# Convolution and SwiGLU on one core: output copies shared by two engines, taps and conversion jobs moved

## The chip, the cores and the metric

The kernel runs on one core of one Trainium2 chip. A core has five engines that run side by side, each with its own queue of instructions in program order: TensorE (PE in the profile; PEld is its weight load), VectorE (DVE), ScalarE (ACT), GpSimd (POOL) and SyncE (SP), which here only issues transfers. PSUM is the small memory into which TensorE writes, SBUF the large one from which it reads; transfers (DMA) run on engines of their own and are issued from SP and POOL.

The metric is device time in microseconds (us), the median of several executions. Before the change it is 792.96 us, over 3 runs from 792.71 to 793.93.

## What is computed

A causal convolution over time with 7 taps, whose weights are a softmax per head, and then a gated feed-forward layer on its output:

```python
def _attn_ref(x, weight):                 # x [8, 4096, 192], weight [8 heads, 7 taps]
    w = np.exp(weight - weight.max(-1, keepdims=True))
    w = w / (w.sum(-1, keepdims=True) + 1e-09)
    x_pad = np.concatenate([zeros(B, 6, D), x], axis=1)
    # out[b, s, head, g] = sum over k of w[head, k] * x_pad[b, s + k, head, g]
    ...

def _moe_ref(x, w_gate, w_val, w_out):    # x [32768, 192], d_ff 1536
    g = x @ w_gate
    silu = g * (1.0 / (1.0 + np.exp(-g)))
    return (silu * (x @ w_val)) @ w_out
```

Inputs and output are float32; the kernel works in float16 with float32 accumulation.

## The kernel before

**Blocks, chunks, steps.** The 32768 tokens are 64 blocks of 512 (`TB`). The feed-forward width of 1536 is 12 chunks of 128. One step of the main loop (line 886) is one chunk of one block: step `n` = 12 x block + chunk `j`, 768 steps. Four blocks are a unit (`u`, 48 steps), 16 units in all.

**A step.** `gate_val(n)` (line 757) multiplies the convolved input `xc[b]` (three tiles of 128 rows, the third dimension `k`) by the weights of that chunk: three pairs of 64-row matmuls, gate and val side by side, into one PSUM tile each, three buffers per name. ScalarE takes `silu` of gate (L775), VectorE multiplies it by val into `h` (L777), 15 buffers.

**Slots.** After chunks 1, 4, 7 and 10 a slot of `down` matmuls (L792) adds `h` times the output weights into two accumulator banks, `acc0` and `acc1`, which have one buffer each. The slot behind chunk 7 (`slot(1)`, 24 matmuls) takes the h of chunks 0 to 5 of its own block, the one behind 10 (36) chunks 0 to 8, the one behind chunk 1 of the next block (24) chunks 6 to 11, the one behind chunk 4 (12) chunks 9 to 11. With this last one the block is done: ScalarE copies both banks to `o_sb` (L850, L851), and SP stores it (L854). So the newest h that a slot needs is that of two steps before, and the slot behind 4 needs none that is new.

**Where the convolved input comes from.** Units 0, 1, 4, 7, 10 and 13 are convolved on TensorE, with a band matrix (`conv_half`, two halves of 32 matmuls, each in a slot behind chunk 10; for unit 1 at steps 25 and 31; unit 0 by smaller pieces at the start), casts to SBUF, a store to a scratch in DRAM and transposing fetches (`fetch`, L520, three per block). The others (`POOLED`: 2, 3, 5, 6, 8, 9, 11, 12, 14, 15) are convolved tap by tap on the other engines. `cast_x` writes a unit's input as float16 to DRAM (POOL's queue, L586), `turn_x` reads it back transposed (SP's queue, L601; 528 columns, two names of tiles with 6 buffers each), `join_x` puts two halves into one tile (L605). Six jobs make a unit (`conv_job`): block 0, pair 0, block 1, pair 1, block 2, block 3. A job is 7 taps: ScalarE writes the first into `total` and another into `part` (L676), VectorE adds two to `total` (`dve_step`, L651), and then GpSimd adds the part and the last three (L641, L626), and writes the result. `place` (L700) copies the results of jobs into the tiles `t1` and `t2` of a block by four SP transfers.

**What sets the order.** Everything is written out by hand: `seq` keeps the order of calls on each engine. `planned` (line 716) gives each unit the steps for its cast, its turns and its jobs: units 2 and 3 by a table, the others 118 and 95 steps before their first. `pooled_work` (line 732) runs at the end of each step: VectorE's next tap behind chunks 4 and 10, and behind 1 and 7 when VectorE's job is behind ScalarE's; ScalarE's next tap behind chunks 1, 7 and 10, up to two jobs ahead of VectorE. A block is placed 14 steps after its last job was issued and not before 16 steps ahead of its use. An instruction's place in its queue is what these steps fix; when it runs, its waits decide. SP and POOL have no tie to a step other than such waits.

**Tap weights per channel.** `make_picks` (step 24) makes two selection masks of 8 x 128 with GpSimd iotas and four VectorE operations; `make_channel_taps` (step 33) uses them in four small matmuls and one ScalarE copy into `both_taps`.

Of the kernel before, what the change touches and what calls it, by code (L numbers as in the profile page):

```python
# [10 lines left out]
def kernel(  # L11
# [9 lines left out]
    nc = tc.nc  # L21
    fp32 = mybir.dt.float32
    fp16 = mybir.dt.float16
    i32 = mybir.dt.int32
    AF = mybir.ActivationFunctionType
    ALU = mybir.AluOpType
# [5 lines left out]
    H, K = weight.shape  # L32
    NT = B * S
    Dff = moe_w_gate.shape[1]
    P = 128
    Q = 64
    SL = D // Q
    grp = D // H
    SUBS = 4
    TB = P * SUBS  # L40
# [32 lines left out]
    def seq(i):  # L73

        e = i.ins.engine
        if e in last_on:
            tc.add_manual_dep(i.ins, last_on[e].name, NOSYNC, reason="order")
        last_on[e] = i.ins
        return i

    wpool = ctx.enter_context(tc.tile_pool(name="wts", bufs=1))
    cpool = ctx.enter_context(tc.tile_pool(name="conv", bufs=2))
# [29 lines left out]
    def xe_tile(e):  # L112
        xe[e] = cpool.tile([P, 6, D], fp16, tag="xe", name="xe", bufs=4)
# [62 lines left out]
    def load_wo(m):  # L176
        seq(
            nc.gpsimd.dma_start(
                out=wo16[:, E * m : E * m + E, :].rearrange("p e d -> p (e d)"),
                in_=moe_w_out[WF * m : WF * m + WF, :].rearrange(  # L180
                    "(p e) d -> p (e d)", p=P
                ),
            )
        )

    def small(name, shape, dt=fp32):
        return wpool.tile(shape, dt, tag=name, name=name)
# [14 lines left out]
    load_w(2)  # L202
    for m in range(3):
        load_wo(m)
    xe_tile(2)
    xe_load(2)
    xe_tile(3)
# [32 lines left out]
    def make_shift(n):  # L240
# [26 lines left out]
            op=ALU.mult,  # L267
# [8 lines left out]
            op0=ALU.mult,  # L276
            op1=ALU.subtract,
# [249 lines left out]
    XP = 16  # L527
# [6 lines left out]
    pick = {}  # L534

    def make_picks():
        for name, first, rows in (("c01", 0, P), ("c2", P, Q)):
            which = small(f"which_{name}", [H, P], i32)
            seq(
                nc.gpsimd.iota(  # L540
                    which,
                    pattern=[[0, P // rows], [1, rows]],
                    base=first,
                    channel_multiplier=-grp,
                )
            )
            low = small(f"low_{name}", [H, P])
            seq(nc.vector.tensor_single_scalar(low, which, 0, op=ALU.is_ge))
            pick[name] = small(f"pick_{name}", [H, P], fp16)
            seq(  # L550
                nc.vector.scalar_tensor_tensor(
                    pick[name], which, float(grp), low, op0=ALU.is_lt, op1=ALU.mult
                )
            )

# [40 lines left out]
    def turn_x(u, i, at):  # L596
        rows = xs[u][TB * i : TB * i + TB + XP]
        tiles = (x01, x12)[at // Q]
        tag = f"x{at // Q}"
        t = cpool.tile([P, TB + XP], fp16, tag=tag, name=tag, bufs=6)  # L600
        seq(nc.sync.dma_start_transpose(out=t, in_=rows[:, at : at + P]))  # L601
        tiles[u, i] = t

# [111 lines left out]

    def planned(v):
        s0 = ustep * v
        cast, jobs = {2: (19, 44), 3: (40, 60)}.get(v, (s0 - 118, s0 - 95))
        turns = (
            (0, 0), (0, Q), (2, Q), None, (1, 0), (1, Q), (3, Q), None, (2, 0), (3, 0)  # L720
        )
        lead = {2: (33, 1), 3: (49, 1)}.get(v, (cast + 7, 2))
        plan.setdefault(cast, []).append(lambda: cast_x(v))
        for m, turn in enumerate(turns):
            if turn:
                todo = lambda turn=turn: turn_x(v, *turn)
            else:
                todo = lambda i=m // 4: join_x(v, i)
            plan.setdefault(lead[0] + lead[1] * m, []).append(todo)
        plan.setdefault(jobs, []).append(lambda: queue_jobs(v))  # L730

    def pooled_work(n, j, busy):
        step_now[0] = n
        if not busy:
            ready = dve_steps[0][0] if dve_steps else None
            ahead = act_steps[0][0] if act_steps else n_jobs[0]
            if ready is not None and (
                j in (4, 10) or (j in (1, 7) and ready < ahead)
            ):
                dve_steps.pop(0)[1]()  # L740
            if j in (1, 7, 10) and act_steps and (ready is None or ahead < ready + 3):
                act_steps.pop(0)[1]()
        while placing:
            u, i = placing[0]
            need = (u, "block", i), (u, "pair", i % 2)
            if not all(job in finished for job in need):
                break
            done = max(finished[job] for job in need)
            if n < max(done + 14, ustep * u + NCH * i - 16):
                break  # L750
            placing.pop(0)
            place(u, i)
# [27 lines left out]
    acc = {}  # L780
# [44 lines left out]
    def slot(k, b, after=None, between=None):  # L825

        if k == 1:
            acc[b] = [
                apool.tile([P, 2, D], fp32, tag=f"acc{i}", name=f"acc{i}")
                for i in range(2)  # L830
            ]
            down(b, [(False, G[0])], 1, after)
            if between is not None:
                between()
            down(b, [(False, G[1])], 1, None)
        elif k == 2:
            down(b, [(True, G[0]), (True, G[1])], 0, after)
            if between is not None:
                between()
            if b < n_blocks - 1:  # L840
                down(b, [(False, G[2])], 0, None)
        elif k == 3:
            down(b, [(True, G[2])], 1, after)
            if between is not None:
                between()
            down(b, [(False, G[3])], 1, None)
        else:
            down(b, [(True, G[3])], 0, after)
            o_sb = hpool.tile([P, SUBS, D], fp32, tag="o_sb", name="o_sb", bufs=3)
            seq(nc.scalar.copy(o_sb[:, 0:2, :], acc[b][0]))  # L850
            seq(nc.scalar.copy(o_sb[:, 2:4, :], acc[b][1]))  # L851
            t0 = b * TB
            seq(
                nc.sync.dma_start(  # L854
                    out=out[t0 : t0 + TB, :].rearrange("(s p) d -> p s d", p=P),
                    in_=o_sb,
                )
            )
            del acc[b]
# [26 lines left out]
    for n in range(n_steps):  # L886
        b, j = divmod(n, NCH)
        u, ls = divmod(n, ustep)
        work = None
        if n in (12, 19):  # L890

            def work(e=2 if n == 12 else 3):
                early(e, (gate_bank, gate_bank, val_bank))

        at = (25, 31) if u == 0 else (10, 22)
        if u + 1 < NU and not pooled(u + 1) and ls in at:

            def work(u=u, hh=at.index(ls)):
                conv_half(u + 1, hh)

        gate_val(n)
        if n == 6:
            early(1, (*acc_banks, gate_bank))
        elif n == 8:
            eturn(1, (*acc_banks, gate_bank))
        elif n in (9, 12, 15, 17):
            k = {9: 1, 12: 2, 15: 3, 17: 4}[n]
            slot(k, 0, silu[n - 1 if k == 4 else n - 2], work)
        elif j % 3 == 1 and n > 18:
            k = {1: 3, 4: 4, 7: 1, 10: 2}[j]  # L910
            slot(k, b - 1 if j < 7 else b, silu[n - 2], work)
        if n == 18:
            eturn(2, (*acc_banks, gate_bank))
        elif n == 20:
            eout(3)
        elif n == 21:
            efetch(3)
        if n == 24:
            make_picks()
        if n == 33:  # L920
            make_channel_taps()
        for job in plan.pop(n, ()):
            job()
        pooled_work(n, j, work is not None)
        if u + 1 < NU and not pooled(u + 1):
            if ls == at[0]:
                conv_dup(u + 1)
            if ls == at[1]:
                for m in range(2):
                    conv_out(u + 1, m)  # L930
            if ls == at[1] + 1:
                for m in range(2, 8):
                    conv_out(u + 1, m)
            lo = 32 if u == 0 else 28
            if ls in range(lo, lo + 12, 3):
                fetch(UB * (u + 1) + (ls - lo) // 3)
        if u + 2 < NU and not pooled(u + 2):
            if ls == (21 if u == 0 else 1):
                x16_tile(u + 2)
                load_x(u + 2, 0, silu[n - 1])  # L940
            if ls == (23 if u == 0 else 5):
                load_x(u + 2, 1, silu[n - 1])
            if ls == (37 if u == 0 else 26):
                dup_x(u + 2)
    b = n_blocks - 1
# [41 lines left out]
```

## Time and profile before

| | |
|---|---|
| median of 3 runs | 792.96 us |
| the profiled execution | 793.59 us |
| its span, from the first instruction to the last | 791.8 us |
| TensorE clock granted in it | 0.999 |
| busy: PE, DVE, ACT, POOL | 775.6, 638.4, 588.6, 500.7 us |

The profile is one execution. A busy share is a mean over the whole span, so stretches with different limits are mixed in it: units with tap jobs load DVE, ACT and POOL, the others hardly load POOL. The page's groups give, per line of the kernel, the engine, the shapes out<-in, the count, the busy time, the mean duration of one in ns, and the idle time of the engine just before such an instruction with what ended most of it. The chain is the work that ended last, followed back from the end: each piece has its start, its length, its engine and line, and x and the number of instructions merged in it. A timeline lists one engine's instructions with start and length, and in square brackets the idle time before and what ended it; for SP the length is that of issuing the transfer, not of moving the data. All times count from the start of the span.

### The profile page before, as it was taken

To read this page: it belongs to the slowest core of one execution; us is meant where nothing else is said; L and a number is where in the kernel's file an instruction comes from. 1 tells how busy PE (TensorE), PEld (TensorE's weight loads), DVE (VectorE), ACT (ScalarE), POOL (GpSimd) and SP (SyncE) were. 2 spreads that over 40 slices of the span, in tenths; PEclk is the share of its full clock that TensorE was granted. 3 is DMA by queue.
4 is the path that set the end of the run, shared out by engine and by line. 5 is a ranking of instruction groups with operands and counts; after the bars stand their busy time and mean duration, and the time that the engine had idled before them with its cause. 6 is when DMAs were issued, how large, how long until landed. Compare 5 with 4: busy or idle time off the path is not lost.

```text
span 791.8 us, 27799 instructions
## 1 busy us (share of the span) xinstructions
PE 775.6 (98%) x11371; PEld 521.7 (66%) x11371; DVE 638.4 (81%) x949; ACT 588.6 (74%) x1054; POOL 500.7 (63%) x485
## 2 busy tenths in 40 slices
PE   8999999999999999999999999999999999999997
PEld 5666666666666666666666666666666666666665
DVE  6677889888888867888896688898767888886665
ACT  6677787877878767777876678788668787876664
POOL 8102999996899920589995047899802689990000
PEclk9999999999999999999999999999999999999999
DMA  9965538355642394386129638631862653221211
GB/s 140 177 141 99 124 106 166 83 123 129 115 109 69 56 201 109 94 130 133 39 68 174 117 83 155 107 92 46 146 144 78 150 123 76 68 64 40 68 55 41
DMA packets 159840, 83.90 MB, mean 106 GB/s; under 512 B 102552, under 2 KB 159136, under 8 KB 159136
## 3 DMA queue, kind: packets, MB, share of 16 engines
q1 hardware_dynamic: 139216, 65.58, 35.4%
q0 software_dynamic: 20496, 16.54, 15.0%
q8 instruction: 89, 1.46, 0.8%
q14 instruction: 39, 0.32, 0.1%
HBM read 33.08 MB, written 38.60 MB: 91 GB/s over the span
## 4 chain that ended last, share of the span: by engine, by line
PE 94%; DVE 2%; issue 1%; SPq 1%; DMA 0%; ACT 0%; DVEq 0%; ACTq 0%
PE gate L766 60%; PE acc L792 30%; DVE h L777 2%; PE val L766 2%; PE cv L462 1%; PE warm L867 1%; DMA x<-xs 0%; SPq L520 0%; PE turn L431 0%; PE cv L373 0%; SPq L498 0%; PE acc L813 0%; ACT tme L391 0%; ACT wide L331 0%; ACT sig L775 0%
## 5 line engine op out<-in xcount | busy, mean ns | idle before, releaser
L777 DVE TENSOR_TENSOR h<-sig,val 128x512 f16<-128x512 f16 x768 | 500.0, 685 | 143.5 <-PE val L766 123.1
L775 ACT ACTIVATE sig<-gate 128x512 f16<-128x512 f32 x768 | 455.3, 599 | 183.0 <-PE val L766 155.9
L766 PEld LDWEIGHTS <-w 64*128 64x128 f16 x4608 | 255.6, 110 | 182.3 <-issue 1.5
L766 PE MATMUL val<-pxc,w 64*128 64x512 f16 x1440 | 337.2, 376 | 0.0
L766 PE MATMUL gate<-pxc,w 64*128 64x512 f16 x1440 | 337.2, 376 | 0.0
L792 PE MATMUL acc<-wo,h 64*128 64x192 f16 x6096 | 300.4, 243 | 9.8 <-DVE h L777 7.9
L792 PEld LDWEIGHTS <-h 64*128 64x128 f16 x6096 | 257.7, 94 | 73.9 <-DVE h L777 13.3
L766 PE MATMUL val<-xc,w 64*128 64x512 f16 x864 | 203.6, 376 | 0.3 <-DVE h L777 0.3
L766 PE MATMUL gate<-xc,w 64*128 64x512 f16 x864 | 203.6, 376 | 0.0
L626 POOL TENSOR_TENSOR total<-total,piece 128x512 f32<-128x512 f32 x120 | 158.4, 1320 | 10.0
L641 POOL TENSOR_SCALAR piece<-x,both_taps 128x512 f32<-128x512 f16 x180 | 146.1, 812 | 0.0
L651 DVE SCALAR_TENSOR_TENSOR total<-x,both_taps,total 128x512 f32<-128x512 f16 x120 | 130.4, 1087 | 0.0
L626 POOL TENSOR_TENSOR total<-total,part 128x512 f32<-128x512 f32 x60 | 81.0, 1349 | 69.6 <-DVE total L651 53.9
L490 POOL COPY tm<-tm 128x1280 f16<-128x1280 f16 x5 | 6.2, 1249 | 125.5 <-DVE tm L479 125.5
L626 POOL TENSOR_TENSOR pxc<-total,piece 128x512 f16<-128x512 f32 x40 | 55.8, 1396 | 3.3
L676 ACT ACTIVATE total<-x,both_taps 128x512 f32<-128x512 f16 x60 | 42.8, 714 | 2.6 <-DMA x<-xs 2.6
L676 ACT ACTIVATE part<-x,both_taps 128x512 f32<-128x512 f16 x60 | 42.8, 714 | 0.0
L851 ACT COPY o_sb<-acc 128x384 f32<-128x384 f32 x63 | 30.6, 486 | 0.0
L850 ACT COPY o_sb<-acc 128x384 f32<-128x384 f32 x63 | 30.2, 479 | 0.1
L626 POOL TENSOR_TENSOR y<-total,piece 128x512 f16<-128x512 f32 x20 | 25.7, 1287 | 1.7
L479 ACT CAST tm<-cv 128x480 f16<-128x480 f32 x20 | 10.2, 562 | 6.8 <-PE cv L462 6.8
L479 DVE CAST tm<-cv 128x480 f16<-128x480 f32 x20 | 12.2, 651 | 0.5
(68 smaller groups left out, 88.4 us busy)
## 6 DMA issues: line engine op xcount, KB each, us to landing
out_dram<-o_sb SPq DMA_DIRECT2D x63, 384.0 KB
pxc<-pxc SPq DMA_DIRECT2D x80, 64.0 KB
pxc<-y SPq DMA_DIRECT2D x80, 64.0 KB
x<-in_x_dram POOLq DMA_DIRECT2D x10, 480.0 KB, 9.7
scr<-tm SPq DMA_DIRECT2D x35, 130.0 KB
xs<-in_x_dram POOLq DMA_DIRECT2D x5, 774.0 KB, 7.0
xs<-in_x_dram POOLq DMA_DIRECT2D x5, 768.0 KB, 10.4
x<-x SPq DMA_DIRECT2D x8, 480.0 KB
```

The costliest lines, as they stand in the source:

```text
L462: nc.tensor.matmul(banks[r][32 * c : 32 * c + 32, t * w : t * w + w], band[Q * r : Q * r + Q, h, :], x16[u][Q * r : Q * r + Q, NG * c : NG ...
L479: eng(tm[u][:, NG * r : NG * r + NG, 2 * grp * hp : 2 * grp * hp + 2 * grp].rearrange("p g (t e) -> p g t e", t=2), banks[r][:, 0 : 2 * w] ...
L626: nc.gpsimd.tensor_tensor(job["dst"] if k == K - 1 else total, total, part, op=ALU.add)
L641: nc.gpsimd.tensor_scalar(part, shifted(k), scalar1=job["tap"][:, k : k + 1], scalar2=1.0, op0=ALU.mult, op1=ALU.mult,)
L651: nc.vector.scalar_tensor_tensor(job["total"], shifted(k), job["tap"][:, k : k + 1], job["total"], op0=ALU.mult, op1=ALU.add,)
L676: nc.scalar.activation(part, shifted(k), AF.Copy, scale=job["tap"][:, k : k + 1])
L766: nc.tensor.matmul(o, w16[m][p0 : p0 + Q, k, e::E], xc[b][k][p0 : p0 + Q, 0:TB], start=(k == 0), stop=(k == SL - 1),)
L775: silu[n] = seq(nc.scalar.activation(sg, g, AF.Silu)).ins
L777: seq(nc.vector.tensor_tensor(hj, sg, v, op=ALU.mult))
L792: nc.tensor.matmul(acc[b][bank][:, s, :], hj[p0 : p0 + Q, ts(2 * bank + s, P)], wo16[p0 : p0 + Q, j, :], start=(not second and j == 0 and ...
L850: seq(nc.scalar.copy(o_sb[:, 0:2, :], acc[b][0]))
L851: seq(nc.scalar.copy(o_sb[:, 2:4, :], acc[b][1]))
```

## The change

Five edits:

- **Output copy.** Of the two copies of a finished block's banks, the second goes from ScalarE to VectorE (`nc.vector.tensor_copy`), for the 63 blocks before the last.
- **Taps.** VectorE's taps stand behind chunks 1, 7 and 10, whenever one is ready; none behind chunk 4. ScalarE's condition is as before.
- **Picks.** The two iotas of `make_picks` and the first compare, now on GpSimd, move to the loads at the start, ahead of the input of blocks 2 and 3 and unit 1. What is left (two VectorE operations) moves from step 24 to 34, `make_channel_taps` from 33 to 37.
- **Steps of the jobs.** Unit 2: cast 19 to 21, first turn 33 to 42, jobs 44 to 54. Unit 3: cast 40 to 50, first turn 49 to 60 with two steps between turns in place of one, jobs 60 to 72. All others: 6 steps later.
- **Buffers.** The transposed input has 8 buffers per name in place of 6.

```diff
--- before.py
+++ after.py
@@ -202,6 +202,20 @@
     load_w(2)
     for m in range(3):
         load_wo(m)
+    which = {}
+    above = {}
+    for name, first, rows in (("c01", 0, P), ("c2", P, Q)):
+        which[name] = small(f"which_{name}", [H, P], i32)
+        seq(
+            nc.gpsimd.iota(
+                which[name],
+                pattern=[[0, P // rows], [1, rows]],
+                base=first,
+                channel_multiplier=-grp,
+            )
+        )
+        above[name] = small(f"above_{name}", [H, P])
+        seq(nc.gpsimd.tensor_single_scalar(above[name], which[name], 0, op=ALU.is_ge))
     xe_tile(2)
     xe_load(2)
     xe_tile(3)
@@ -534,22 +548,12 @@
     pick = {}
 
     def make_picks():
-        for name, first, rows in (("c01", 0, P), ("c2", P, Q)):
-            which = small(f"which_{name}", [H, P], i32)
-            seq(
-                nc.gpsimd.iota(
-                    which,
-                    pattern=[[0, P // rows], [1, rows]],
-                    base=first,
-                    channel_multiplier=-grp,
-                )
-            )
-            low = small(f"low_{name}", [H, P])
-            seq(nc.vector.tensor_single_scalar(low, which, 0, op=ALU.is_ge))
+        for name in which:
             pick[name] = small(f"pick_{name}", [H, P], fp16)
             seq(
                 nc.vector.scalar_tensor_tensor(
-                    pick[name], which, float(grp), low, op0=ALU.is_lt, op1=ALU.mult
+                    pick[name], which[name], float(grp), above[name],
+                    op0=ALU.is_lt, op1=ALU.mult,
                 )
             )
 
@@ -597,7 +601,7 @@
         rows = xs[u][TB * i : TB * i + TB + XP]
         tiles = (x01, x12)[at // Q]
         tag = f"x{at // Q}"
-        t = cpool.tile([P, TB + XP], fp16, tag=tag, name=tag, bufs=6)
+        t = cpool.tile([P, TB + XP], fp16, tag=tag, name=tag, bufs=8)
         seq(nc.sync.dma_start_transpose(out=t, in_=rows[:, at : at + P]))
         tiles[u, i] = t
 
@@ -715,11 +719,11 @@
 
     def planned(v):
         s0 = ustep * v
-        cast, jobs = {2: (19, 44), 3: (40, 60)}.get(v, (s0 - 118, s0 - 95))
+        cast, jobs = {2: (21, 54), 3: (50, 72)}.get(v, (s0 - 112, s0 - 89))
         turns = (
             (0, 0), (0, Q), (2, Q), None, (1, 0), (1, Q), (3, Q), None, (2, 0), (3, 0)
         )
-        lead = {2: (33, 1), 3: (49, 1)}.get(v, (cast + 7, 2))
+        lead = {2: (42, 1), 3: (60, 2)}.get(v, (cast + 7, 2))
         plan.setdefault(cast, []).append(lambda: cast_x(v))
         for m, turn in enumerate(turns):
             if turn:
@@ -734,9 +738,7 @@
         if not busy:
             ready = dve_steps[0][0] if dve_steps else None
             ahead = act_steps[0][0] if act_steps else n_jobs[0]
-            if ready is not None and (
-                j in (4, 10) or (j in (1, 7) and ready < ahead)
-            ):
+            if j in (1, 7, 10) and ready is not None:
                 dve_steps.pop(0)[1]()
             if j in (1, 7, 10) and act_steps and (ready is None or ahead < ready + 3):
                 act_steps.pop(0)[1]()
@@ -848,7 +850,7 @@
             down(b, [(True, G[3])], 0, after)
             o_sb = hpool.tile([P, SUBS, D], fp32, tag="o_sb", name="o_sb", bufs=3)
             seq(nc.scalar.copy(o_sb[:, 0:2, :], acc[b][0]))
-            seq(nc.scalar.copy(o_sb[:, 2:4, :], acc[b][1]))
+            seq(nc.vector.tensor_copy(o_sb[:, 2:4, :], acc[b][1]))
             t0 = b * TB
             seq(
                 nc.sync.dma_start(
@@ -915,9 +917,9 @@
             eout(3)
         elif n == 21:
             efetch(3)
-        if n == 24:
+        if n == 34:
             make_picks()
-        if n == 33:
+        if n == 37:
             make_channel_taps()
         for job in plan.pop(n, ()):
             job()
```

In the changed kernel a line's number is up to 14 higher than before (L601 becomes L605, L777 becomes L779).

## Prediction

> **What bounds the kernel.** The page's table of engines comes first, then the chain that ended last and the costliest groups.
>
> ```profile
> PE 775.6 (98%) x11371; PEld 521.7 (66%) x11371; DVE 638.4 (81%) x949; ACT 588.6 (74%) x1054; POOL 500.7 (63%) x485
> ...
> PE 94%; DVE 2%; issue 1%; SPq 1%; DMA 0%; ACT 0%; DVEq 0%; ACTq 0%
> ...
> L777 DVE TENSOR_TENSOR h<-sig,val 128x512 f16<-128x512 f16 x768 | 500.0, 685 | 143.5 <-PE val L766 123.1
> ...
> L651 DVE SCALAR_TENSOR_TENSOR total<-x,both_taps,total 128x512 f32<-128x512 f16 x120 | 130.4, 1087 | 0.0
> ...
> L851 ACT COPY o_sb<-acc 128x384 f32<-128x384 f32 x63 | 30.6, 486 | 0.0
> ```
>
> PE sets the end at full clock, so only what makes PE wait counts. The chain in order of time, blocks 27 to 29, shows where:
>
> ```profile
> 352.27 1.49 PE acc L792 x36
> 355.70 0.99 PE acc L792 x24
> 358.63 0.49 PE acc L792 x12
> 361.16 0.47 issue
> 361.63 0.69 DVE h L777
> 362.36 0.34 PE acc L792 x4
> 364.64 1.49 PE acc L792 x36
> ```
>
> The x36 piece comes once a block (behind chunk 10). Undisturbed, it returns after 11.73 us; here after 12.37, since the slot behind chunk 7 waited for the h of chunk 5. DVE's timeline has a 1.81 us tap at 359.90, behind chunk 4. I took the start of every step (first gate matmul in PE's timeline) and compared each chunk with its undisturbed length (0.65 us; 1.64 with the slots behind 1 and 7, 1.14 behind 4, 2.13 behind 10). From block 5 on, every excess over 0.06 us, apart from the 32-matmul convolution halves (0.64 each), is at chunk 7 and follows a tap behind chunk 4 longer than 1.165 us: 24 cases, 12.1 us together. One more, 1.27 us, lies at step 49: ScalarE's first tap of unit 2 waits for its transpose, and the silu behind it in its queue waits too.
>
> ```profile
> 64.81 0.72 ACT L676 ACTIVATE total<-x,both_taps 128x512 f32<-128x512 f16 x1 [2.64 <-DMA x<-xs]
> ```
>
> SyncE's timeline shows that transpose issued at 60.88, behind three for block 4. Later it shows how close unit 3 runs:
>
> ```profile
> 57.05 3.74 SPq L520 DMA_TRANSPOSE xc<-scr  x3
> 60.88 4.54 SPq L601 DMA_TRANSPOSE x<-xs  x3
> ...
> 156.34 3.78 SPq L601 DMA_TRANSPOSE x<-xs  x3
> 161.69 0.47 SPq L605 DMA_DIRECT2D x<-x  x1
> 162.26 0.96 SPq L854 DMA_DIRECT2D out_dram<-o_sb  x1
> 163.32 3.85 SPq L601 DMA_TRANSPOSE x<-xs  x3
> 167.28 0.52 SPq L700 DMA_DIRECT2D pxc<-pxc  x1
> 167.85 1.23 SPq L700 DMA_DIRECT2D pxc<-y  x2
> 169.13 0.59 SPq L700 DMA_DIRECT2D pxc<-pxc  x1
> ```
>
> **What the Trainium skill says.** "SBUF — State Buffer", Who interferes with whom: a VectorE instruction with two SBUF inputs and a GpSimd one that reads SBUF exclude each other for a whole instruction; VectorE with one SBUF input outside its two-port modes does not contend. The trace agrees: taps take 0.739 us to 1.827, h (one PSUM input) 0.668 to 0.690 throughout. "VectorE: DVE Perf Modes", the section on the TRN2 errata, prices a 384-element copy from PSUM at 120+384 cycles of 0.96 GHz, an estimate of 0.525 us; the one that this trace has (L952) took 0.557, which I use. "PSUM — Partial Sum Buffer", Engine vs sequencer instructions: ScalarE's queue is strict FIFO; the 2.64 us above held the silu.
>
> **The change, part by part.** The order of instructions of the changed kernel gives the positions.
>
> *No tap behind chunk 4.* The 24 stalls go: −12.1 us. The 120 taps now stand 44 behind chunk 1, 40 behind 7 and 36 behind 10 (before: 24, 16 and 36, with 44 behind 4).
>
> *Taps behind chunk 1.* In blocks 58 to 61 h starts 1.47 us after its step and frees VectorE 0.61 later. A tap of length d behind chunk 1 lets the next h start at 2.00+d; it is wanted at 1.64+1.47=3.11, so d over 1.11 makes it late. Val has three PSUM buffers, so step 5 takes that of step 2: h ends 2.16 after its step, step 5 starts 2.44 after step 2, the release takes 0.06: 0.22 to spare. A tap there costs d−1.34 (the longest in the trace, 1.314, cost nothing). Behind 7 and 10 the following slots leave more room: 1.827 behind 10 cost nothing. Which d come is unknown, since they depend on where GpSimd stands. Mean excess over 1.34: all 120 taps 9.3 us, 0.077 each; those behind 1, none; those behind 4, 7.9 us over 44, 0.179 each. For 44 taps: 0 to 7.9 us; I take the general mean, +3.4, as nothing says which phase of GpSimd they will meet.
>
> *Second output copy on VectorE.* It issues behind h of chunk 4, at 2.08; the slot's 12 matmuls are over at 1.14. It frees VectorE at 2.56, and the next h is wanted at 1.14+1.47=2.61. Cost 0; the cover is VectorE's wait for the next val. The bank is free at 2.64, wanted at 3.09. ScalarE loses 63 x 0.37 us of slack work: 0. VectorE per block: 12 h at 0.60 issue to issue, 3 taps at about 1.0, a copy 0.48, 10.7 of 11.73.
>
> *Picks.* Two GpSimd iotas (0.21 each) and two compares (not in the trace; between the iota's 0.2 and a full 128x512 operation's 0.69) go ahead of the last loads: 0.8 to 1.8 us later. xe of step 12 lands at 19.8 and is read at 22.06: hidden. VectorE's four operations, 0.98 us at step 24, made steps 25 and 26 0.12 and 0.47 too long; two remain behind chunk 10, where the slot covers them. With the lighter ScalarE at step 28: −0.7 (0 to −0.9).
>
> *Jobs of unit 2 later.* The wait at step 49 goes (−1.3), but its transposes now stand behind all twelve of unit 1's. SyncE from 57.05: four triples at their own lengths (3.83, 3.97, 4.27, 4.19 to the next row) and an output store (0.64) make 16.9: issue at 73.95, landing 2.7 later (third transpose of the 156.34 row to the join behind it, 2.8), 76.65. ScalarE reaches the tap at step 55, about 70.9, and waits. Tap 0.65 and silu 0.58 and release: the slot behind step 58 can start at 77.95. Undisturbed it would at 73.74−1.27+0.65=73.12. Stall 4.8, less 0.3 since the loads behind SyncE's start come forward a little more than PE does: +4.5 (3.5 to 6).
>
> *Jobs of unit 3 later.* GpSimd's job for (3, block 1) ends at 149.77 now, at once followed by the cast of unit 5, landing 6.6 later; SyncE's next transpose waits for it and then, in the rows above, 10.9 us pass before the placing of block 13. Its last landing is 1.95 after issue, 171.1, wanted at 172.5+0.4: 1.8 to spare. In the changed order the same sequence stands, but that job's last tap moves from step 118 to 127, and the cast stays behind the job. Steps 118 to 156 took 38.8; 127 to 156 take 29 chunks, 29.2, a convolution half 0.64, stalls 0.2: 30.05. GpSimd's lag: eight jobs at 8.1 us and 2.6 of loads after a first start 3.15 behind step 61; its job ends 15.0 behind step 127, against 16.0 behind 118. So 8.7−1.0=7.7 is lost, less 1.8: +5.8 at step 156 (2 to 7.5 for jobs of 7.6 to 8.3 us). Units 5 to 15 have over 50 us to spare, so their 6 steps cost 0. Two more transpose buffers only remove waits: 0.
>
> **Sum.** −12.1+3.4−0.7−1.3+4.5+5.8=−0.4: span 791.8 to 791.4. Around it lie 1.8 (793.59−791.8), so 793.2 for the profiled execution. That one stood 0.63 over the median of 792.96, so 792.6.
>
> **Rivals.** (a) One new wait is missing or small, because SyncE or GpSimd is further ahead than I count: 788.1 without step 58's, 786.8 without step 156's. For it: each hangs on lengths of a queue. Against: both come from waits that the trace shows. (b) Neither comes: −10.7, 782.3. (c) Slower: taps behind chunk 1 meet GpSimd as those behind chunk 4 did, 0.179 each, 7.9 us: 797.1. GpSimd is 95 to 100% busy in these blocks; against it, taps behind 1 have been short so far. It decides from 5.4 us, 0.12 a tap, where the sum passes +1.6. That the change doesn't move the stalls at all is ruled out by the order.
>
> **From cases to numbers.** The forecast 0.50 (its own range 789.5 to 795.5), (a) 0.17, (b) 0.04, (c) 0.29. Within 0.2% (1.6 us, what a measurement of this kernel can tell) is 791.4 to 794.5. Of the forecast's 0.50, 0.15 lies below, 0.25 inside, 0.10 above. Faster 0.36, same 0.25, slower 0.39. Leaving out (b) and the top of (c), whose upper end also takes in step 156 at 7.5: 786 to 797.5.
>
> **What would show it.** No chunk 7 longer than 1.64; excess at chunk 4, on val behind h, where a tap behind 1 exceeds 1.34; copies of 0.56 on VectorE however busy GpSimd is; a 5 us idle of ScalarE on x<-xs near 71 to 77; PE waiting for pxc at the start of block 13. Wrong if ScalarE doesn't wait there, if block 13 starts on time, or if copies stretch.

## The result, and the profile after

| | before | after |
|---|---|---|
| median, us | 793.44 (792.71 to 793.97, 4 runs) | 798.58 (797.65 to 799.22, 4 runs) |
| the profiled execution, us | 793.59 | 798.3 |
| its span, us | 791.8 | 796.5 |
| TensorE clock granted in it | 0.999 | 0.991 |

The changed kernel takes 1.0064 of the time before, 95% interval 1.0047 to 1.0082: slower by 0.64%, where 792.6 was forecast from 792.96. The page of the changed kernel: engines, TensorE's two rows of the 40 slices, and the engines of the chain that ended last.

```profile
PE 778.7 (98%) x11371; PEld 608.4 (76%) x11371; DVE 670.0 (84%) x1010; ACT 579.9 (73%) x991; POOL 503.7 (63%) x487
...
PE   8997999988999999999999999999999999999997
...
PEclk9998999998999999999999999999999999999999
...
PE 88%; POOL 8%; issue 1%; DVE 1%; DMA 1%; ACT 0%; SPq 0%; POOLq 0%; ACTq 0%
```

TensorE has holes in the fourth slice and in the ninth and tenth, and the granted clock is not full in the fourth and the tenth. The chain has 8% of GpSimd that it did not have. The groups of the page:

```profile
L779 DVE TENSOR_TENSOR h<-sig,val 128x512 f16<-128x512 f16 x768 | 501.8, 684 | 116.3 <-PE gate L768 75.2
...
L655 DVE SCALAR_TENSOR_TENSOR total<-x,both_taps,total 128x512 f32<-128x512 f16 x120 | 131.0, 1091 | 0.0
...
L853 DVE COPY o_sb<-acc 128x384 f32<-128x384 f32 x63 | 34.6, 549 | 0.0
L852 ACT COPY o_sb<-acc 128x384 f32<-128x384 f32 x63 | 30.3, 480 | 0.2
```

h and the taps are as long as before; the second output copy takes 549 ns on VectorE. The chain in order of time, where the kernel before stalled:

```profile
350.44 1.42 PE acc L794 x33
...
362.17 1.42 PE acc L794 x33
```

From one block to the next 11.73 us, the undisturbed length; before, 12.37 stood here. The stalls of chunk 7 are gone. The view of waits (total, times, longest) has these new ones:

```profile
ACT total L680 <- DMA x<-xs: 7.0, 2, 6.6
...
PE acc L794 <- ACT sig L777: 5.6, 1, 5.6
PE gate L768 <- DMA pxc<-pxc: 5.3, 1, 5.3
```

They are the two waits of the forecast. The first, in ScalarE's and then SyncE's timeline:

```profile
67.16 1.89 ACT L777 ACTIVATE sig<-gate 128x512 f16<-128x512 f32 x3 [0.17 <-PE val L768]
75.66 0.72 ACT L680 ACTIVATE total<-x,both_taps 128x512 f32<-128x512 f16 x1 [6.60 <-DMA x<-xs]
```

```profile
54.76 12.82 SPq L534 DMA_TRANSPOSE xc<-scr  x9
67.68 0.53 SPq L856 DMA_DIRECT2D out_dram<-o_sb  x1
68.31 4.60 SPq L534 DMA_TRANSPOSE xc<-scr  x3
73.00 3.82 SPq L605 DMA_TRANSPOSE x<-xs  x3
```

Unit 2's first transposes go out at 73.00, behind all twelve of unit 1. The windows over this stretch (PE, PEld, DVE, ACT, POOL busy, then the granted clock, DMA share, GB/s) show what follows the wait:

```profile
70.00:74.00 4.00, 1.36 (x14) 0.47 (x10) 0.00 (x0) 0.00 (x0) 0.00 (x0) 1.00 1.01 113
74.00:76.00 2.00, 0.00 (x0) 0.00 (x0) 0.00 (x0) 0.34 (x1) 0.00 (x0) 0.85 0.47 98
76.00:78.00 2.00, 1.08 (x14) 1.01 (x16) 1.11 (x2) 2.00 (x5) 0.00 (x0) 0.50 0.51 105
78.00:80.00 2.00, 2.00 (x28) 1.78 (x26) 1.44 (x3) 0.44 (x1) 0.00 (x0) 0.50 0.15 34
80.00:82.00 2.00, 2.00 (x12) 0.69 (x10) 0.08 (x1) 0.60 (x1) 0.00 (x0) 0.50 0.46 99
82.00:86.00 4.00, 4.00 (x56) 2.48 (x54) 3.22 (x5) 2.99 (x5) 0.74 (x1) 0.97 0.32 72
```

TensorE works again from 76.92, but at half clock until just after 82. The same in the chain: the 36-matmul slot that took 1.48 us a block earlier takes 3.06.

```profile
59.63 1.48 PE acc L794 x36
...
76.92 3.06 PE acc L794 x36
```

The second wait is at the start of block 13; SyncE's timeline and the windows:

```profile
170.72 2.66 SPq L605 DMA_TRANSPOSE x<-xs  x2
...
175.38 4.48 SPq L605 DMA_TRANSPOSE x<-xs  x3
179.96 0.52 SPq L704 DMA_DIRECT2D pxc<-pxc  x1
180.59 1.18 SPq L704 DMA_DIRECT2D pxc<-y  x2
181.81 0.59 SPq L704 DMA_DIRECT2D pxc<-pxc  x1
```

```profile
178.00:180.00 2.00, 0.00 (x0) 0.00 (x0) 0.00 (x0) 0.00 (x0) 2.00 (x2) 1.00 0.36 77
180.00:182.00 2.00, 0.07 (x1) 0.07 (x1) 0.00 (x0) 0.00 (x0) 1.92 (x3) 0.80 0.55 121
182.00:184.00 2.00, 1.80 (x5) 0.39 (x6) 0.00 (x0) 0.14 (x1) 1.92 (x3) 0.50 0.54 140
```

The place of block (3,1) (block 1 of unit 3, which is block 13), at 179.96, stands behind unit 5's transposes; TensorE goes on at 181.93, and again runs at half clock, to 188.0. Its first four matmuls after the wait start one by one, each some 2 us after the issue of one of the place's four transfers:

```profile
181.93 0.58 PE L768 MATMUL gate<-pxc,w 64*128 64x512 f16 x1 [5.28 <-DMA pxc<-pxc]
182.64 0.58 PE L768 MATMUL val<-pxc,w 64*128 64x512 f16 x1
183.24 0.58 PE L768 MATMUL gate<-pxc,w 64*128 64x512 f16 x1
183.87 0.58 PE L768 MATMUL val<-pxc,w 64*128 64x512 f16 x1
```

The table cuts the profiled executions by the first gate matmul of steps 48, 72, 156 and 168:

| stretch | before, us | after, us | difference |
|---|---|---|---|
| start of the span to step 48 | 63.51 | 61.59 | -1.92 |
| blocks 4 and 5 | 25.20 | 31.77 | +6.57 |
| blocks 6 to 12 | 83.83 | 82.91 | -0.92 |
| block 13 | 12.94 | 21.55 | +8.61 |
| blocks 14 to 63, to the end of the arithmetic | 602.73 | 595.13 | -7.60 |

Blocks 4 and 5, whose undisturbed length is 23.46, hold 5.56 us of idle TensorE and 2.75 more; block 13, undisturbed 12.37 with its convolution half, holds 5.48 of idle and 3.70 more. The slot above took twice its time at half clock, so half of the time that TensorE worked there is lost: 76.92 to 82.2, so 2.65. In block 13 the transfers, and not the clock, set the pace until 183.87. From there the half clock costs 2.0 (steps 157 to 167 take 13.95, against 11.72 in the experiment with 34 idle matmuls, where the clock is full, and 0.2 of that difference is a longer convolution half). The other 1.5 of block 13's 3.70 passes while the four transfers land one after another.

### The profile page after: what moved, and what is told of

The parts are those of the page before. It is cut to its first block, busy times and chain, and to the rows that moved or that the text cites. A ratio compares the mean times of both kernels' runs of the same rounds, so it can differ in the third digit from the quotient of the medians.

```text
span 796.5 us, 27870 instructions
## 1 busy us (share of the span) xinstructions
PE 778.7 (98%) x11371; PEld 608.4 (76%) x11371; DVE 670.0 (84%) x1010; ACT 579.9 (73%) x991; POOL 503.7 (63%) x487
## 4 chain that ended last, share of the span: by engine, by line
PE 88%; POOL 8%; issue 1%; DVE 1%; DMA 1%; ACT 0%; SPq 0%; POOLq 0%; ACTq 0%
PE val L768 37%; PE acc L794 29%; PE gate L768 20%; POOL total L630 4%; POOL piece L645 3%; DVE h L779 1%; PE cv L476 1%; POOL pxc L630 0%; POOL y L630 0%; PE warm L869 0%; PE turn L445 0%; DMA x<-xs 0%; PE cv L387 0%; POOL x L98 0%; PE acc L815 0%
## 5 line engine op out<-in xcount | busy, mean ns | idle before, releaser
L779 DVE TENSOR_TENSOR h<-sig,val 128x512 f16<-128x512 f16 x768 | 501.8, 684 | 116.3 <-PE gate L768 75.2
L777 ACT ACTIVATE sig<-gate 128x512 f16<-128x512 f32 x768 | 458.3, 597 | 190.9 <-PE gate L768 135.3
L768 PEld LDWEIGHTS <-w 64*128 64x128 f16 x4608 | 345.1, 110 | 139.5 <-issue 12.7
L794 PE MATMUL acc<-wo,h 64*128 64x192 f16 x6096 | 334.0, 244 | 5.6 <-ACT sig L777 5.6
L794 PEld LDWEIGHTS <-h 64*128 64x128 f16 x6096 | 304.4, 94 | 35.4 <-ACT sig L777 6.5
L630 POOL TENSOR_TENSOR total<-total,piece 128x512 f32<-128x512 f32 x120 | 163.4, 1361 | 10.0
L630 POOL TENSOR_TENSOR pxc<-total,piece 128x512 f16<-128x512 f32 x40 | 52.8, 1319 | 3.3
L853 DVE COPY o_sb<-acc 128x384 f32<-128x384 f32 x63 | 34.6, 549 | 0.0
L852 ACT COPY o_sb<-acc 128x384 f32<-128x384 f32 x63 | 30.3, 480 | 0.2
```

The lines of the kernel that those rows point to most:

```text
L630: nc.gpsimd.tensor_tensor(job["dst"] if k == K - 1 else total, total, part, op=ALU.add)
L768: nc.tensor.matmul(o, w16[m][p0 : p0 + Q, k, e::E], xc[b][k][p0 : p0 + Q, 0:TB], start=(k == 0), stop=(k == SL - 1),)
L777: silu[n] = seq(nc.scalar.activation(sg, g, AF.Silu)).ins
L779: seq(nc.vector.tensor_tensor(hj, sg, v, op=ALU.mult))
L794: nc.tensor.matmul(acc[b][bank][:, s, :], hj[p0 : p0 + Q, ts(2 * bank + s, P)], wo16[p0 : p0 + Q, j, :], start=(not second and j == 0 and ...
L853: seq(nc.vector.tensor_copy(o_sb[:, 2:4, :], acc[b][1]))
```

## Experiments

The kernel before, measured beside each, had medians of 792.84 to 793.16. A stall is told as the length of a step in the profile over its undisturbed length.

**The steps of the jobs, taken out and put in alone.** The changed kernel with the four lines of steps as before:

```diff
-cast, jobs = {2: (21, 54), 3: (50, 72)}.get(v, (s0 - 112, s0 - 89))
+cast, jobs = {2: (19, 44), 3: (40, 60)}.get(v, (s0 - 118, s0 - 95))
-lead = {2: (42, 1), 3: (60, 2)}.get(v, (cast + 7, 2))
+lead = {2: (33, 1), 3: (49, 1)}.get(v, (cast + 7, 2))
```

> The changed kernel with the steps of casts, turns and jobs as before the change (all units); the shared copies, the tap positions, the picks and the 8 buffers stay. Theory: both waits (step 58, block 13) are gone, the stalls of chunk 7 too: 793.4 less 12.1, plus 2 for taps behind chunk 1, less 1.9 at the start: 781 to 783. Rival: the gain after block 13 comes from the later jobs, not from the tap positions, and the copies on VectorE cost: 790 or more.

Measured: 782.55 (780.94 to 784.75, 4 runs), ratio 0.987 (0.9841 to 0.9899), as the theory has it. The opposite, the kernel before with only the changed steps and the 8 buffers:

> The kernel before with the new steps of casts, turns and jobs and the 8 buffers alone; copies, tap positions and picks as before. Theory: the two waits come with their clock, +6 to 7 in block 4 and +8 to 9 in block 13, while the stalls behind chunk 4's taps stay: 806 to 810. Rival: the waits come from the shared copies or from the tap order, and the steps alone cost less than 4: under 797.5.

Measured: 804.5 (803.85 to 805.63), ratio 1.0146 (1.0123 to 1.017). Both waits are in its trace (5.26 us of idle TensorE in block 4; 4.1 in block 13, which is 7.63 over its undisturbed length), and the clock goes to half for 6.83 us after each; 9.8 us of chunk 7's stalls remain. It came out 1.5 us under the range expected. So the steps alone cost 11 to 12 us, and the other edits alone gain 10 to 11. The kernel with the old steps beats both the kernel before and the changed one. The two do not add up: their sum is a loss of 1.3, and together they lose 5.1. Most of the rest lies in blocks 14 to 63. There the steps alone gain 2.4, the other edits 9.6, and both together 7.6 and not 12.0, since the steps alone already remove 2.2 of chunk 7's stalls, which the taps then cannot remove again.

**Is it the half clock?** Idle 128x512 matmuls (24, about 5.4 us) ahead of step 58's own and of step 156's own keep TensorE busy through the waits; they compute nothing that is used:

```diff
+for _ in range(24 if n in (58, 156) else 0):
+    seq(nc.tensor.matmul(g, fill, fill.unsqueeze(1).to_broadcast([P, SUBS, P]),
+        start=True, stop=True, skip_group_check=True))
```

> The changed kernel with 24 idle matmuls (128x512, 0.21 us each, 5.1 us) written into the gate tile of steps 58 and 156 ahead of its own matmuls, so that TensorE has work while it waits. Nothing of the computation changes. Theory: of the time lost in blocks 4, 5 and 13, some 6.4 us is TensorE at half clock for 6.8 us after each wait of 5.5 us; filled, the clock stays at 1.0, the waits end at the same moment, and the time falls by 5 to 6.5 us to 792 to 793.6. Rival: the time after the waits goes to refilling ScalarE's and VectorE's queues, and the idle matmuls change nothing or add: 798 to 800.

Measured: 796.84 (794.42 to 799.99, 9 runs), ratio 1.005 (1.0029 to 1.007). Between the two expectations, so the windows of its trace:

```profile
76.00:78.00 2.00, 2.00 (x13) 0.77 (x13) 0.00 (x0) 0.64 (x2) 0.00 (x0) 1.00 0.63 133
```

```profile
182.00:184.00 2.00, 0.61 (x2) 0.22 (x2) 0.00 (x0) 0.00 (x0) 1.92 (x3) 1.00 0.44 98
184.00:186.00 2.00, 1.65 (x8) 0.61 (x8) 0.31 (x1) 0.60 (x1) 2.00 (x2) 0.62 0.79 228
186.00:188.00 2.00, 2.00 (x26) 1.73 (x22) 1.24 (x3) 1.21 (x2) 0.40 (x1) 0.53 0.65 143
```

Where the matmuls covered the wait, ScalarE still waited 6.5 us for its transpose, the clock stayed full and blocks 4 and 5 took 29.09 in place of 31.77: 2.7 us less. At block 13 they ended before the place had landed; 2.19 us of idle and a half-clock stretch of 3.41 us followed. The granted clock of the nine runs tells that this differs between executions: five, from 794.42 to 796.84, had 0.999 or 1.0, and four, from 798.8 to 799.99, had 0.997. The two groups' medians lie 3.6 us apart, more than 3.41 us at half clock can cost (1.7), so the clock isn't the whole difference. With 34 of them there:

> The changed kernel with idle 128x512 matmuls ahead of step 58's own (24) and of step 156's own (34, about 7.3 us). They keep TensorE busy in both waits and change no result. Theory (each wait costs half clock after it, 6.4 us together, beside its idle time): 791.5 to 794, no half-clock stretch inside, block 4 near 17.3 us and block 13 with the matmuls near 19. Rival (the time beyond my sum has another cause, transfers or queues that are late after the waits): 797 to 800.

Measured: 795.99 (795.49 to 796.89), ratio 1.004 (1.0025 to 1.0055). The clock is full throughout, as the theory has it, and blocks 4 and 5 take 28.87, 2.9 less than in the changed kernel. But the total misses its range by 2 us. Now the matmuls were too many: the place's first transfer was issued at 178.52, in the changed kernel 1.97 us passed from there to the first matmul (179.96 to 181.93), so that block 13 could have gone on at 180.5; it did at 182.40. Blocks 12 and 13 together took 32.46 in place of 34.07. The half clock behind step 58 is thereby shown at 2.7 to 2.9 us. The kernel with unit 5's cast moved (below) has the same program up to there; its blocks 4 and 5 took 32.63 with 6.46 of idle, so it too lost 2.7 beyond its idle time. That behind step 156 is 2.0, from steps 157 to 167 of the two profiles as told above; in the filled kernel the transfers had landed before, so the landings are out of that comparison.

**Block 13: what stands in the way.** Unit 5's cast at step 122 in place of 128 (turns stay at 135, jobs at 151), so that it stands ahead of GpSimd's job for (3, block 1):

```diff
-cast, jobs = {2: (21, 54), 3: (50, 72)}.get(v, (s0 - 112, s0 - 89))
+cast, jobs = {2: (21, 54), 3: (50, 72), 5: (122, 151)}.get(v, (s0 - 112, s0 - 89))
-lead = {2: (42, 1), 3: (60, 2)}.get(v, (cast + 7, 2))
+lead = {2: (42, 1), 3: (60, 2), 5: (135, 2)}.get(v, (cast + 7, 2))
```

> The changed kernel with the cast of unit 5 at step 122 in place of 128, its turns and jobs where they are. The cast then stands before the job of (3, block 1) in GpSimd's queue, some 8 us earlier. Theory: SyncE's transposes of unit 5 no longer hold the placing of block 13 back; block 13 takes 12.4 us in place of 21.55, the total falls by 8 to 9.2 us to 789.4 to 790.6. Rival: GpSimd's job of pair 1 of unit 3 itself is late, and block 13 still waits 4 us or more: 794 or more.

Measured: 791.5 (789.85 to 794.0, 12 runs), ratio 0.9984 (0.9971 to 0.9997). Block 13 takes 14.04, with 1.02 of idle and no half clock; block 4 keeps its wait and its half clock. About 7 us gone, 1 less than expected. Unit 5's transposes still stand ahead of the place, but it goes out at 176.18, 3.4 us before block 13 begins; in the changed kernel it went out 3.7 after. Then unit 2's row alone as before, in the changed kernel:

```diff
-cast, jobs = {2: (21, 54), ...
+cast, jobs = {2: (19, 44), ...
-lead = {2: (42, 1), ...
+lead = {2: (33, 1), ...
```

> The changed kernel with unit 2's row of steps as before (cast 19, turns from 33, jobs 44), unit 3's and all others as changed. Theory (jobs run one after another, so that unit 2's later jobs push those of unit 3: both waits come from unit 2's row): step 58's wait is gone with its half clock (8.3 us), step 49's comes back (1.3), and block 13's wait shrinks to 2 us or less with no half clock: 783 to 786. Rival (block 13's wait comes from unit 3's own row, as the prediction has it): 790 to 792.5, with 5 us idle at block 13.

Measured: 787.34 (786.94 to 789.02), ratio 0.9933 (0.9919 to 0.9948), between the two. Step 58's wait is gone, step 49's is back (1.33). GpSimd's ninth job, the one named in the prediction, ends at 149.19 in place of 162.20, although unit 3's own row was left as changed: jobs run one after another, and unit 2's row had pushed unit 3's. Block 13 idles 2.33 in place of 5.48. But it loses 5.06 in all, and its windows show one reason, the half clock:

```profile
172.00:174.00 2.00, 0.74 (x2) 0.22 (x2) 0.61 (x1) 0.00 (x0) 2.00 (x2) 1.00 0.42 98
174.00:176.00 2.00, 1.45 (x15) 0.94 (x15) 0.58 (x1) 0.79 (x2) 0.13 (x1) 0.96 0.46 100
176.00:178.00 2.00, 2.00 (x25) 1.83 (x22) 1.46 (x3) 1.02 (x2) 0.00 (x0) 0.50 0.51 107
```

Unit 5's cast, fixed at step 128, now stands behind GpSimd's tenth job and goes out at 157.19 (162.15 in the changed kernel), so its transposes are still ahead of the place. TensorE idles 1.50, 0.28, 0.33 and 0.23 us, and the clock goes to half for 3.41 us all the same, which the expectation had left out. This profile is of the longest of the four runs (789.02); the two shortest, 786.94 and 786.99, had a granted clock of 0.999 against its 0.998, so that they probably did without it.

The kernel with the old steps lost 1.91 at step 156. With unit 5's turns moved behind the place of block (3,1):

```diff
-{2: (19, 44), 3: (40, 60)}
+{2: (19, 44), 3: (40, 60), 5: (128, 163)}
-{2: (33, 1), 3: (49, 1)}
+{2: (33, 1), 3: (49, 1), 5: (143, 2)}
```

> The changed kernel with the steps of casts, turns and jobs as before, but unit 5's cast at step 128, its turns from 143 and its jobs at 163, so that the place of block (3,1) stands ahead of unit 5's transposes on SyncE. Theory (what holds block 13 up is only those transposes, not the job of GpSimd, whose last one for this block ends 14 us earlier): the 1.9 us at step 156 that the kernel with the old steps still loses are gone, no stall over 0.3 us from step 48 on: 780 to 781.5, against 782.55. Rival (the place waits for the job or for its own transfers): 782.3 or more, with the wait at step 156.

Measured: 782.19 (781.25 to 783.48), ratio 0.9857 (0.9835 to 0.988). The median is 0.7 over the range expected and not apart from 782.55, and step 49 still stalls (1.57), which the expectation had overlooked: the profile of the kernel with the old steps, the same program up to there, has no stall at step 49, so this wait comes in one execution and not in the other. Of block 13 it shows what the theory says. SyncE's timeline:

```profile
153.84 0.46 SPq L704 DMA_DIRECT2D pxc<-pxc  x1
157.34 1.10 SPq L704 DMA_DIRECT2D pxc<-y  x2
158.49 2.76 SPq L704 DMA_DIRECT2D pxc<-pxc  x1
166.34 3.77 SPq L605 DMA_TRANSPOSE x<-xs  x3
```

The place is out at 161.25, 10 us before block 13 begins, and the block takes its undisturbed 12.37. Last, unit 2's jobs in that kernel at step 50 in place of 44:

> The kernel with the old steps and unit 5 late (782.19), and one more edit: unit 2's jobs at step 50 in place of 44, so that ScalarE's first tap stands at step 55 in place of 49 and its transpose has landed. Theory (step 49's wait is all that this tap costs, and the chain of jobs has 6 steps to spare before block 13): no stall at step 49 (1.57 us in that profile), no new one at step 55 nor at block 13, 780 to 781.5. Rival (the chain of jobs is then late again): a wait of 2 us or more at block 12 or 13, 783 or more.

Measured: 781.82 (781.14 to 782.21), ratio 0.9856 (0.9839 to 0.9872). No stall at step 49, which one profile alone does not prove to be the edit's doing, but 1.13 at step 156 and 0.27 at step 96 came in its place: the jobs are late again, by half of what the rival asks. It has the lowest median of all, by less than these runs can tell.

**Taps, copy and picks one by one.** The kernel before with VectorE's taps moved alone:

```diff
-if ready is not None and (
-    j in (4, 10) or (j in (1, 7) and ready < ahead)
-):
+if j in (1, 7, 10) and ready is not None:
```

> The kernel before with one edit: VectorE's taps behind chunks 1, 7 and 10 in place of 4. Theory (the taps alone carry the gain, the price of the copy on VectorE is 0 and the picks are worth under 1 us): 782.5 to 784.5, no excess at chunk 7, a few stalls of step 5 of (length of the tap behind chunk 1 minus 1.53 us), 1 to 3 us in sum. Rival (the lighter ScalarE or the picks carry part of it): 787 or more.

Measured: 786.27 (785.0 to 786.53), ratio 0.9913 (0.9898 to 0.9928): between the two. No stall at chunk 7 and 1.87 us of stalls in step 5; but also 1.66 at step 156, where the kernel before had none, and five of the eight convolution halves cost 0.78 to 0.82 in place of 0.64, 0.9 together. Neither was expected, and the cause of the second stays open. The copy alone, with the taps where they were:

```diff
-seq(nc.scalar.copy(o_sb[:, 2:4, :], acc[b][1]))
+seq(nc.vector.tensor_copy(o_sb[:, 2:4, :], acc[b][1]))
```

> The kernel before with one edit: the second output copy on VectorE, taps stay behind chunk 4. Theory (the copy costs 0 only because VectorE then waits for the next val; with a tap queued behind it that cover is gone): every tap behind chunk 4 starts 0.48 us later, so it stalls the slot behind chunk 7 from a length of 0.69 us on in place of 1.165; over the 44 taps of the profile before that is 27.8 us in place of 12.1, so 806 to 810. Rival (a copy on VectorE costs nothing wherever it stands): 792 to 794.

Measured: 802.56 (802.17 to 803.07), ratio 1.0123 (1.0106 to 1.014). A loss of 9.7 us, not 14. VectorE's timeline:

```profile
361.98 1.94 DVE L777 TENSOR_TENSOR h<-sig,val 128x512 f16<-128x512 f16 x3
363.84 0.55 DVE L851 COPY o_sb<-acc 128x384 f32<-128x384 f32 x1
364.30 1.45 DVE L651 SCALAR_TENSOR_TENSOR total<-x,both_taps,total 128x512 f32<-128x512 f16 x1
```

The tap starts behind the copy, as expected, and stalls at chunk 7 are 21.5 us in place of 12.0. The threshold of 0.69 was right: the 44 lengths less 0.69 sum to 22.0. What was wrong is the lengths, since the taps behind chunk 4 became shorter, 1.189 us in the mean against 1.323. The copy put back on ScalarE in the kernel with the old steps:

> The changed kernel with the steps as before and the second output copy back on ScalarE (taps, picks and buffers as changed). Theory (the copy costs nothing on either engine while no tap stands behind chunk 4): 782 to 783.5, the same as with the copy on VectorE (782.55). Rival (the lighter ScalarE is what made the difference between 786.27 with the taps alone and 782.55): 785.5 to 787.

Measured: 785.99 (784.47 to 786.6), ratio 0.9902 (0.9883 to 0.9921). So the rival's number holds: the copy on VectorE in place of ScalarE is worth 3.4 us in the medians, of four runs each, whose ranges just overlap. In the profiles 2.4 us of it is found: ten taps behind chunk 1 over 1.53 us in place of three, 3.42 us of stalls in step 5 in place of 1.07. The copy on VectorE costs nothing there, and other taps are long. Whether that comes from the lighter ScalarE or from the copy's own place in VectorE's queue is not separated, since the edit moves one instruction from the one to the other. This kernel has the changed picks and the 8 buffers, and without them, with the taps alone, it took 786.27: so these two together are worth nothing that can be told. The picks alone (the first, second and last hunks of the diff):

> The kernel before with one edit: iotas and compares on GpSimd with the loads, picks at step 34, channel taps at 37. Theory of the prediction (-0.7): 791.9 to 792.6, the 0.6 us at steps 25 and 26 gone. Rival (the picks shift the start itself, and are what separates 786.27 from 782.55): 788.5 to 790.

Measured: 792.59 (791.75 to 794.77, 13 runs), ratio 0.9996 (0.9986 to 1.0005): no difference that can be told. The stalls of steps 25 and 26 fall from 0.59 to 0.13, but steps 22 and 36 lose 1.67 in that profile, against 0.91 before.

## Why the prediction was wrong

The waits came where it put them; what was left out is the clock after them. The step that failed is the price of the two new waits, +4.5 at step 58 and +5.8 at step 156: each was counted as waiting time alone, and TensorE's clock behind it at nothing. The profile has waits of 5.6 and 7.0 us, 2.3 more than counted, and behind them 2.65 and 2.0 us of half clock. Of the 6.0 us by which the median missed, 5.1 lie in the profiled span; the other 0.9 is where the profiled execution stands to its median, 0.63 above it before and 0.28 below it after. Point by point, in us of the profiled span:

| step of the sum | predicted | measured |
|---|---|---|
| chunk 7 | -12.1 | -12.1 |
| taps behind chunk 1 | +3.4 | +1.8 |
| front | -0.7 | -1.9 |
| step 49 | -1.3 | -1.3 |
| step 58, wait | +4.5 | +5.6 |
| step 156, wait to the last landing | +5.8 | +7.0 (5.5 of it idle) |
| half clock after both | 0 | +4.7 |
| steps with a convolution half | 0 | +0.9 |
| sum | -0.4 | +4.7 (span: +4.7) |

- **Chunk 7** was right: no step with chunk 7 is longer than undisturbed, and the taps alone gain 6.6 us (786.27), with the copy, the picks and the buffers 10 to 11.
- **Taps behind chunk 1.** Their excess over 1.34 summed to 3.5, expected 3.4; that is chance, as the forecast said itself that nothing told which lengths would come (in the other kernels with these taps it is 1.4 to 5.9). The threshold was not right. Behind chunk 1 a tap of length d costs d-1.53, not d-1.34, and it is step 5 that is longer. VectorE's timeline of the changed kernel, at a stall of 0.24:

```profile
343.07 1.79 DVE L655 SCALAR_TENSOR_TENSOR total<-x,both_taps,total 128x512 f32<-128x512 f16 x1
344.78 1.87 DVE L779 TENSOR_TENSOR h<-sig,val 128x512 f16<-128x512 f16 x3
346.57 0.54 DVE L853 COPY o_sb<-acc 128x384 f32<-128x384 f32 x1
347.04 1.86 DVE L779 TENSOR_TENSOR h<-sig,val 128x512 f16<-128x512 f16 x3
```

  The sum of d-1.53 gives 1.79 for the changed kernel, 1.08 with the old steps, 3.42 with the copy back and 1.87 with the taps alone; their stalls were 1.81, 1.07, 3.42 and 1.87. The working let val's bank be wanted when step 5 begins, 2.44 after step 2. In the traces a tap of 1.48 has val start at 2.57 with step 5 no longer than else, and one of 1.79 at 2.88 with step 5 longer by 0.26: val can come nearly 0.2 late at no cost. Rival (c) did not come; that its 797.1 is near to what was measured is chance.
- **The output copy.** 549 ns and no cost of its own was right, and only because no tap follows it (with one, 9.7 us lost). That the move of the copy is worth 0 in all was wrong with the old steps: 3.4 us. What it is worth with the changed steps was not measured apart.
- **Front.** The changed kernel reached step 48 at 61.59 in its profile. Three experiments whose program is the same up to there reached it at 63.40, 63.08 and 63.66. So the -1.9 is mostly that one execution (theirs is within 0.5 of the 63.51 before), and the -0.7 of the picks was not found by themselves either.
- **Step 58** ended nearly as worked out: unit 2's transposes at 73.00 against 73.95 in the working. ScalarE reached the tap 1.85 sooner (69.05 against 70.9), so the wait is longer.
- **Step 156** is right in place, and its chain too (job, cast, SyncE's transposes, place). The wait to the last landing came out 1.2 longer: GpSimd's job ended 15.9 behind step 127 and not 15.0, and the rest is small. (The working's own last step, 7.7 less 1.8, is 5.9 and not 5.8.) That the idle time alone, 5.5, lies near 5.8 is chance, since TensorE goes on at the first landing. The wait was put under the jobs of unit 3; the run with unit 2's row shows that this row brings most of it. And the six later steps of units 5 to 15, put at 0, are not free for unit 5: its cast alone six steps back takes 7 us off.
- **Rivals (a) and (b)** are the runs that take one wait or both away: without block 13's 791.5, without step 58's 787.34 (which also shortens block 13's), without both 782.55, where (b) had 782.3. For the first two (a) had 786.8 and 788.1. These kernels differ from the changed one by their steps, so that the nearness of (b) proves little.

## What to carry to other kernels

A wait of TensorE is priced as its idle time plus the half clock that can follow, 2 to 3 us here behind waits of some 5.5 us. A stall that is spread over many short ones can be cheaper than the same time in one piece: before the change, 12 us in 24 stalls left the clock full. When jobs run one after another, moving the first moves all; follow the last of them to its deadline, and look at what stands ahead of its transfers in their queue. What an edit costs can hang on what stands behind it in the queue: the copy lost 9.7 us before a tap and gained 3.4 without one.

## What was not expected of the hardware

The Trainium skill, "TensorE: Matmul & The Clock Gate", Part 1: The HAM clock gate (the "warmup" mystery), says that TensorE's clock is set by windows of 3413 ns that run free of the kernel, goes to half after at least one idle window of about 3.4 us and comes back after a busy one. The traces agree on the windows: every stretch at half clock inside these kernels lasted 3.41 or 6.83 us and began a whole number of 3.413 us after the first record of the clock. They do not agree that a whole window must be idle: with 24 idle matmuls the longest gap was 1.50 us and the gaps together 2.19, and with unit 2's row 1.50 and 2.33, so that no window of 3.41 could be idle throughout, wherever it lay. Idle time of TensorE in such windows, worked out from its timeline, and the clock of the next (each kernel named by its edit; "at the end" marks the window in which TensorE's last matmul of the kernel ends):

| kernel | window, us | idle in it, us | clock in it | clock in the next |
|---|---|---|---|---|
| changed | 71.98 to 75.39 | 3.41 | full | half |
| changed | 177.79 to 181.20 | 3.41 | full | half |
| steps alone | 179.65 to 183.07 | 2.72 | full | half |
| 24 idle matmuls | 181.06 to 184.47 | 2.08 | full | half |
| unit 2's row | 172.44 to 175.86 | 1.37 | full | half |
| unit 2's row | 63.22 to 66.63 | 1.16 | full | full |
| copy back | 171.29 to 174.70 | 1.22 | full | full |
| changed | 174.38 to 177.79 | 1.14 | full | full |
| changed | 181.20 to 184.62 | 0.92 | half | half |
| steps alone | 77.25 to 80.67 | 0.83 | half | half |
| 24 idle matmuls | 184.47 to 187.88 | 0.11 | half | full |
| unit 5 late, at the end | 775.08 to 778.49 | 1.84 | full | full |
| jobs at 50, at the end | 774.53 to 777.94 | 1.72 | full | full |
| copy back, at the end | 778.86 to 782.28 | 1.56 | full | full |

Between these blocks the bound seems to lie between 1.22 and 1.37 us of idle in a window of 3.41, and a window at half clock with 0.83 us idle was not enough to come back. But the last three rows, where TensorE had finished and idle time fills the end of the window, do not fit: 1.56 to 1.84 us left the next window at full clock. So the sum of idle time in the windows as drawn here does not decide. All windows of the 14 profiles would fit one bound, near 1.5 to 1.7 us, if the time that counts ended some 0.25 to 0.7 us before the clock changes; this was fitted afterwards and is not shown. The windows' place against the kernel differs from run to run, which fits the two groups of runs of the kernel with 24 idle matmuls. Where exactly the bound lies, and whether work at half clock counts less, stays open.
